# Seven half-size products for one group of weight columns in the first strip, with its operand sums made during the weight conversion

## The chip, the cores and the metric

The kernel runs on one core of one Trainium2 chip. The metric is the time of one execution on the device in microseconds (us). Engines: PE does matrix products into the PSUM banks, DVE, ACT and POOL work elementwise, SP issues transfers (DMA). Each engine works through its own queue in order, and waits at an instruction until what it needs has been signalled.

## The reference, cut to what matters

```python
# q, k, v: (8, 8, 576, 64)
kv = np.einsum('bhsd,bhse->bhde', k, v)
out = np.einsum('bhsd,bhde->bhse', q, kv)
x = out / np.sqrt(np.mean(out * out, axis=-1, keepdims=True) + 1e-06) * g_norm
x = x.transpose(0, 2, 1, 3).reshape(4608, 512)
h = x @ w_in                       # w_in: (512, 2048), 64-bit floats in memory
r = np.maximum(h, 0.0)
out = (r * r) @ w_out              # w_out: (2048, 512), 64-bit floats in memory
```

The weights lie in memory as 64-bit floats and are converted to 32 bits inside the kernel.

## The kernel before

The 4608 tokens are taken in nine strips of 512. For each strip there is a first product (x by w_in, then relu and square into four quarters of g, named 11, 12, 21, 22 in `gq`) and a second one (g by w_out). The attention part for the next strips (the slices that `attend` steps through) runs between the steps.

From the second strip on, products are done by Winograd's form of Strassen's method: 7 products of half-size blocks in place of 8, with sums of blocks as operands. The 7 products of one level are named 1 to 7 and run in the order `ORDER = (1, 2, 6, 5, 7, 3, 4)`; products 1, 6, 7 and 4 accumulate one after the other in bank A, 5 and 3 in bank B, 2 in bank C (`BANK`). Between them `combine` copies the bank on ACT (`snap`, after products 1, 6 and 5) or adds it to an earlier copy on DVE (after 2, 7 and 3), so that a later product into the same bank waits for that copy or sum.

The first strip is different, because its weights are only just arriving. w_in's columns come in four groups (g = 0 to 3). For each group and strip 0 the first product is done plainly, in 4 steps of `up_first`: 4 accumulating matmuls of 128x512 (8 records in the profile, two for each 32-bit matmul), after which ACT drains the bank with a relu and two squares. Four banks rotate (pool `fpsum`).

Beside these 16 steps the weights are converted, pair by pair. A piece is 512 KB of 64-bit numbers in a place of `raw_pool` (two pieces, a pair, to a place). Its way: load by SP (line 248), two ACT operations (`act_words`, lines 260 and 262, of 128x1024), one POOL operation (line 282), two DVE operations (lines 284 and 288). Words between the steps are in pool `wtmp`. `convert_pair(n)` issues the ACT part of pair n+1 ahead, then POOL's and DVE's part of pair n, then further loads, up to `AHEAD` pieces in advance. Pairs 0 to 7 are w_in (two to a group), pairs 8 to 15 w_out; pairs 12 to 15 have four further DVE sums each (`sums_out`), which are stored to memory. `PACE[i]` says how many conversions have been issued after step i. So ACT's queue mixes the drains of steps with the conversions, in the order of the program.

After the 16 steps the pools of the conversion are closed, the pools `stream` and `sum` are opened in their place, and strip 0's second product follows, one level of 7 products (`down`, order 1, 2, 5, 6, 7, 3, 4; lines 865 and 870 are the helpers that issue matmuls). Its operands come from the quarters of g, sums of them made by DVE, and weights partly read back by the transfers `w_blk<-w_out`. During it `sums_in(g)` makes the sums of w_in's blocks for the second strip, with line 316's scaling on ACT and four DVE operations in place (s1, s2, s4 into `w_s`, and a11 - a21 over a21).

Of the kernel before, what the change touches and what calls it, by code (L numbers as in the profile page):

```python
# [10 lines left out]
FP32 = mybir.dt.float32  # L11
# [3 lines left out]
AF = mybir.ActivationFunctionType  # L15
ALU = mybir.AluOpType
# [4 lines left out]
def kernel(  # L21
# [34 lines left out]
    nc = tc.nc  # L56
    P = 128
# [13 lines left out]
    TH = STRIP // 2  # L71
# [4 lines left out]
    SQ = 32  # L76
    Q_ON_PE = 2
    BEHIND = 1.6
    X_ON_PE = 2
    EPS = 1e-6  # L80
    AHEAD = 10
    PACE = (3, 4, 4, 5, 6, 7, 8, 9, 10, 11, 12, 13, 13, 14, 15, 16)
    const = ctx.enter_context(tc.tile_pool(name="const", bufs=1))
    wpool = ctx.enter_context(tc.tile_pool(name="wpool", bufs=1))
# [3 lines left out]
    xn_pool = ctx.enter_context(tc.tile_pool(name="xn", bufs=3))  # L88
    small = ctx.enter_context(tc.tile_pool(name="small", bufs=3))
    g_pool = ctx.enter_context(tc.tile_pool(name="g", bufs=4))  # L90
    dram = ctx.enter_context(tc.tile_pool(name="dram", bufs=1, space=bass.MemoryType.DRAM))
    c_pool = ctx.enter_context(tc.tile_pool(name="c", bufs=6))
    conv = ExitStack()
    xt_pool = conv.enter_context(tc.tile_pool(name="xt", bufs=1))
    raw_pool = conv.enter_context(tc.tile_pool(name="raw", bufs=5))
    spare_pool = conv.enter_context(tc.tile_pool(name="spare", bufs=1))
    wtmp = conv.enter_context(tc.tile_pool(name="wtmp", bufs=2))
    psums = ExitStack()
    fpsum = psums.enter_context(tc.tile_pool(name="fpsum", bufs=4, space=bass.MemoryType.PSUM))
    opening = ExitStack()  # L100
# [116 lines left out]
    KH, FH, DH = NP // 2, d_ff // 2, d_model // 2  # L217
    FQ = FC // 2
    WN = 512
    NG = FQ // 2  # L220
# [3 lines left out]
    block = lambda b: w_in[:, :, :, b] if b < 4 else w_s[:, :, :, b - 4]  # L224
# [14 lines left out]
    raw = []  # L239
# [65 lines left out]
    def minus(eng, out, a, b):  # L305
        eng.tensor_tensor(out=out, in0=a, in1=b, op=ALU.subtract)  # L306
# [3 lines left out]
    def pieces_in(i):  # L310
        g, k = divmod(i // 2, KH)
        convert_pair(i // 2, w_in[:, k, g].rearrange("p (a b) e -> p a (b e)", a=2))

    def sums_in(g):

        nc.scalar.activation(w_in[:, :, g, 0:4], w_in[:, :, g, 0:4], AF.Copy, scale=g_col)
        a11, a21, a12, a22, s1, s2, s4 = (block(b)[:, :, g] for b in range(7))
        nc.vector.tensor_tensor(out=s1, in0=a21, in1=a22, op=ALU.add)
        minus(nc.vector, s2, s1, a11)
        minus(nc.vector, s4, a12, s2)  # L320
        minus(nc.vector, a21, a11, a21)
# [57 lines left out]
    qT, kvd, x_n, xt = {}, {}, {}, {}  # L379
# [207 lines left out]
        if i == len(ns) - 1 and r:  # L587
            queried.pop()

    first = {}  # L590
    TAG_UP = "ABAC"


# [94 lines left out]
    xc = {}  # L688
# [2 lines left out]
        return xt[s][:, ts(th, TH // SQ), ts(kh, KH), :]  # L691

    def sums_x(s):
        xc[s] = t1, t2, t3, t4 = [
            sum_pool.tile([P, TH // SQ, KH, SQ], FP32, name=f"x_t{i}", tag="sum") for i in range(4)
        ]
# [170 lines left out]
    def product(p, i, lhsT, rhs, n):  # L867

        for k in range(n):
            nc.tensor.matmul(  # L870
                bank[BANK[p]][:, i, :], lhsT=lhsT(k), rhs=rhs(k),
                start=p in (1, 5, 2) and i == 0 and k == 0, stop=k == n - 1, skip_group_check=True,
            )

    def combine(p, c11, c12, c21, c22):

        b = bank[BANK[p]]
        if p in (1, 6, 5):
            snap[p] = c_pool.tile([P, 2, 2 * P], FP32, name=f"snap{p}", tag="c")
            nc.scalar.copy(snap[p], b)  # L880
        elif p == 4:
            c21(b)
        else:
            other, c = {2: (1, c11), 7: (5, c22), 3: (6, c12)}[p]
            c(b, snap[other])

    def quarters(s, g):

        if (s, 11) not in gq:
            for q in (11, 12, 21, 22):  # L890
                gq[s, q] = g_pool.tile([P, FQ, TH], FP32, name="gt", tag="gt")
        return {q: gq[s, q][:, 2 * g : 2 * g + 2, :] for q in (11, 12, 21, 22)}
# [27 lines left out]
    def up(s, g, p):  # L920
        open_bank(p)
        rhs = {
            1: halves(s, 0, 0), 2: halves(s, 1, 0), 3: halves(s, 1, 1),
            4: xc[s][3], 5: xc[s][0], 6: xc[s][1], 7: xc[s][2],
        }[p]
        for i in range(2):
            product(p, i, lambda kc: block(A_IN[p])[:, kc, g, ts(i, P)], lambda kc: rhs[:, :, kc, :], KH)
        dest = quarters(s, g)

        def relu_squared(q):  # L930
            def f(b, a):
                o = dest[q]
                nc.vector.tensor_tensor(out=o, in0=b, in1=a, op=ALU.add)
                nc.vector.scalar_tensor_tensor(out=o, in0=o, scalar=0.0, in1=o, op0=ALU.max, op1=ALU.mult)
            return f

        def last(b):
            nc.scalar.activation(dest[21], b, AF.Relu)
            nc.scalar.activation(dest[21], dest[21], AF.Square)

        combine(p, relu_squared(11), relu_squared(12), last, relu_squared(22))
# [417 lines left out]
    for s in range(N_STRIP):  # L1359
# [7 lines left out]
        if s >= DEEP_UP:  # L1367
            steps = [(0.5, up_slot, (s, slot)) for slot in range(55)]
        elif s == 0:
            steps = [(2, up_first, (g, fh, i)) for g in range(NG) for fh in range(2) for i in range(2)]  # L1370
        else:
            steps = [(1, up, (s, g, p)) for g in range(NG) for p in ORDER]
        n_up = len(steps)
# [9 lines left out]
                goal = min(pair_ends, key=lambda end: abs(end - goal))  # L1383
        total, done = sum(w for w, _, _ in steps), 0
        for i, (w, fn, a) in enumerate(steps):
            if s == 0 and i < n_up:
# [10 lines left out]
                if i == 14:  # L1397
                    for b in range(2):
                        store_first(b)
            elif s == 0 and i == n_up:  # L1400
                convert(len(conversions))
                conv.close()

                stream_pool = ctx.enter_context(tc.tile_pool(name="stream", bufs=6, reuse_waits="tile"))
# [56 lines left out]
            n = i + 1 - (n_up - 6)  # L1461
# [41 lines left out]
```

## Time and profile before

| | us |
|---|---|
| median of 3 runs | 869.34 |
| the runs | 869.1, 869.34, 873.36 |
| the profiled execution | 868.8 |
| its span, first to last instruction | 867.0 |
| PE busy in it | 857.8 |
| DVE, ACT, POOL busy | 702.0, 348.9, 328.1 |

The span is what the profile's views divide up; the execution's own time has 1.8 us beside it. The granted PE clock is 1.00 throughout. In the views a line gives the start in us, the duration in us, the engine, the line of the kernel, the operation, output<-input, shape and count, and in brackets the idle time before it with what ended it. Line numbers are those of the kernel before.

### The profile page before, as it was taken

To read this page: it belongs to the slowest core of one execution; us is meant where nothing else is said; L and a number is where in the kernel's file an instruction comes from. 1 tells how busy PE (TensorE), PEld (TensorE's weight loads), DVE (VectorE), ACT (ScalarE), POOL (GpSimd) and SP (SyncE) were. 2 spreads that over 40 slices of the span, in tenths; PEclk is the share of its full clock that TensorE was granted. 3 is DMA by queue.
4 is the path that set the end of the run, shared out by engine and by line. 5 is a ranking of instruction groups with operands and counts; after the bars stand their busy time and mean duration, and the time that the engine had idled before them with its cause. 6 is when DMAs were issued, how large, how long until landed. Compare 5 with 4: busy or idle time off the path is not lost.

```text
span 867.0 us, 32426 instructions
## 1 busy us (share of the span) xinstructions
PE 857.8 (99%) x14176; PEld 804.2 (93%) x14176; DVE 702.0 (81%) x1132; ACT 348.9 (40%) x777; POOL 328.1 (38%) x335
## 2 busy tenths in 40 slices
PE   7999999999999999999999999999999999999998
PEld 6445888889999999999999999999999999999998
DVE  3768988879877996789688967897889777975887
ACT  4888241320048303750356034901491148102810
POOL 1223004630458223730574045704470447145700
PEclk9999999999999999999999999999999999999999
DMA  9898998999999997989698979987678856885583
GB/s 307 277 362 269 274 377 239 295 332 353 280 264 259 342 325 233 228 307 344 209 244 273 341 239 281 283 297 270 198 236 302 301 165 221 293 282 196 175 315 121
DMA packets 169469, 236.46 MB, mean 273 GB/s; under 512 B 78704, under 2 KB 133744, under 8 KB 161008
## 3 DMA queue, kind: packets, MB, share of 16 engines
q1 hardware_dynamic: 169024, 234.33, 83.5%
q8 instruction: 111, 1.82, 0.9%
q14 instruction: 30, 0.25, 0.1%
q10 hardware_dynamic: 304, 0.07, 0.0%
HBM read 197.66 MB, written 36.70 MB: 270 GB/s over the span
## 4 chain that ended last, share of the span: by engine, by line
PE 83%; DMA 7%; DVE 5%; ACT 3%; SPq 1%; issue 1%; DVEq 0%; ACTq 0%
PE ps_A L865 36%; PE ps_B L865 31%; PE ps_C L865 5%; PE ps_A L870 4%; DMA raw<-in_moe_w_in_dram 2%; PE kv_ps L448 2%; PE x_ps L484 2%; PE ps_B L870 2%; DVE w_t L306 1%; DMA w_deep<-w_t 1%; DMA raw<-in_moe_w_out_dram 1%; DMA w_blk<-w_deep 1%; PE ps_C L870 1%; DMA first_qkv<-in_v_dram 1%; ACT w_c L260 1%
## 5 line engine op out<-in xcount | busy, mean ns | idle before, releaser
L865 PE MATMUL ps_B<-w_blk,g_s 128*64 128x128 f32 x2016 | 122.0, 273 | 0.0
L865 PEld LDWEIGHTS ps_B<-w_blk,g_s 128*64 128x64 f32 x2016 | 112.6, 137 | 0.1
L306 POOL TENSOR_TENSOR x_l<-xT 128x256 f32<-128x256 f32 x21 | 16.2, 773 | 230.2 <-PE ps_A L865 230.2
L865 PE MATMUL ps_B<-w_blk,gt 128*64 128x128 f32 x1504 | 94.1, 273 | 0.3 <-DMA w_blk<-w_deep 0.3
L865 PE MATMUL ps_A<-w_blk,g_s 128*64 128x128 f32 x1536 | 92.2, 273 | 0.0
L1323 POOL TENSOR_TENSOR snap<-snap,gt 128x512 f32<-128x512 f32 x35 | 46.2, 1320 | 112.5 <-ACT snap L1328 93.6
L865 PEld LDWEIGHTS ps_A<-w_blk,g_s 128*64 128x64 f32 x1536 | 85.7, 137 | 0.0
L865 PEld LDWEIGHTS ps_B<-w_blk,gt 128*64 128x64 f32 x1504 | 84.6, 137 | 0.8 <-PE ps_B L865 0.5
L1328 ACT COPY snap<-ps_A 128x512 f32<-128x512 f32 x63 | 36.8, 585 | 103.6 <-PE ps_A L865 96.2
L1263 ACT ACTIVATE gt<-gt 128x512 f32<-128x512 f32 x112 | 70.2, 627 | 9.9 <-DVE gt L1323 9.9
L1264 ACT ACTIVATE gt<-gt 128x512 f32<-128x512 f32 x112 | 70.7, 631 | 3.5
L865 PE MATMUL ps_A<-w_blk,gt 128*64 128x128 f32 x1152 | 71.2, 273 | 0.0
L865 PEld LDWEIGHTS ps_A<-w_blk,gt 128*64 128x64 f32 x1152 | 64.7, 137 | 0.0
L1112 ACT COPY o_sb<-ps_A 128x128 f32<-128x128 f32 x24 | 6.4, 265 | 144.7 <-PE ps_A L865 109.4
L306 DVE TENSOR_TENSOR gt<-gt 128x2048 f32<-128x2048 f32 (+1 forms) x29 | 59.7, 2063 | 0.0
L1111 DVE TENSOR_TENSOR o_sb<-o_sb,ps_B 128x256 f32<-128x256 f32 (+1 forms) x123 | 47.4, 386 | 14.3 <-ACT o_sb L1112 9.5
L865 PE MATMUL ps_A<-x_l,w_in 128*64 128x128 f32 x896 | 58.6, 273 | 0.2 <-DVE gt L1323 0.2
L1323 POOL TENSOR_TENSOR gt<-gt,snap 128x512 f32<-128x512 f32 x42 | 52.5, 1279 | 15.1 <-DVE snap L1323 15.1
L865 PEld LDWEIGHTS ps_A<-x_l,w_in 128*64 128x64 f32 x896 | 50.8, 137 | 0.5 <-DVE gt L1323 0.5
L865 PE MATMUL ps_B<-x_l,w_blk 128*64 128x128 f32 x784 | 51.2, 273 | 0.0
L865 PE MATMUL ps_A<-x_l,w_blk 128*64 128x128 f32 x784 | 51.2, 273 | 0.0
L1112 ACT COPY o_sb<-ps_B 128x128 f32<-128x128 f32 x31 | 8.2, 265 | 96.3 <-PE ps_B L865 96.3
(214 smaller groups left out, 1900.2 us busy)
## 6 DMA issues: line engine op xcount, KB each, us to landing
w_blk<-w_deep SPq DMA_DIRECT2D x56, 1024.0 KB, 7.3
w_blk<-w_out SPq DMA_DIRECT2D x56, 768.0 KB, 6.2
w_blk<-w_in_deep SPq DMA_DIRECT2D x49, 768.0 KB, 5.8
raw<-in_moe_w_in_dram SPq DMA_DIRECT2D x16, 512.0 KB, 9.2
raw<-in_moe_w_out_dram SPq DMA_DIRECT2D x16, 512.0 KB, 8.0
k<-in_k_dram SPq DMA_DIRECT2D x29, 256.0 KB, 4.9
v<-in_v_dram SPq DMA_DIRECT2D x29, 256.0 KB, 5.2
x_d<-x_q SPq DMA_DIRECT2D x27, 256.0 KB, 4.8
```

The source lines that it names most:

```text
L260: nc.scalar.activation(c, high_f, AF.Copy, scale=EXPONENT)
L306: eng.tensor_tensor(out=out, in0=a, in1=b, op=ALU.subtract)
L448: nc.tensor.matmul(ps[ts(h, D), i], lhsT=a, rhs=w, start=i == 0 and c == 0, stop=c == C, skip_group_check=True)
L484: nc.tensor.matmul(ps[half, r, i, ts(p, D)], lhsT=q[row, half], rhs=kvd[b, p][row, row], start=True, stop=True)
L865: nc.tensor.matmul(ps[half], lhsT=lhsT[:, half], rhs=rhs, start=start, stop=stop, skip_group_check=True)
L870: nc.tensor.matmul(bank[BANK[p]][:, i, :], lhsT=lhsT(k), rhs=rhs(k), start=p in (1, 5, 2) and i == 0 and k == 0, stop=k == n - 1, skip_gro ...
L1111: add = lambda out, a, b: nc.vector.tensor_tensor(out=out, in0=a, in1=b, op=ALU.add)
L1112: yield nc.scalar.copy(q[:, 3:4], small(1))
L1263: nc.scalar.activation(o, o, AF.Relu)
L1264: nc.scalar.activation(o, o, AF.Square)
L1323: add = lambda eng, out, a, b: eng.tensor_tensor(out=out, in0=a, in1=b, op=ALU.add)
L1328: nc.scalar.copy(t, ps)
```

## The change

Group 2 (`HALVED`) of strip 0's first product is done as seven products instead of four plain steps. Its operands: the four sums of x (`sums_x(0)`) are issued after step 1 and lie in the place where group 3's g will be; the three sums of the group's weights (`first_sums_in`) are issued after step 5, lie in the place of group 2's own g, and a21 is overwritten by a11 - a21 at once, so that `sums_in(2)` later makes its sums from that with three DVE operations. The relu and square of quarter 12 are on ACT instead of DVE.

With 7 steps in place of 4 there are 19 steps; `TURN` maps each to a turn of the former 16, by which the conversions (`PACE`) and other work are placed. A turn that occurs twice issues no conversion the second time: so there is none right after the last step ahead of the group, none after products 2 and 7, and none after the first step of group 3. Inside the group, after products 1, 6, 5, 3 and 4, the conversions of pairs 8, 9, 10, 11 and 12 are issued, each with the ACT part of the pair behind it.

The raw places go from 5 to 6 and the pieces in advance from 10 to 12, the places for words from 2 to 3. The pool `c` (copies of banks and output tiles) is opened only after the conversion; until then copies use the pool `xn`.

```diff
+    HALVED = 2
+    TURN = (*range(7), 6, 7, 7, 8, 9, 9, 10, 11, *range(12, 16))
-    AHEAD = 10
+    AHEAD = 12
-    c_pool = ctx.enter_context(tc.tile_pool(name="c", bufs=6))
     conv = ExitStack()
+    raw_pool = conv.enter_context(tc.tile_pool(name="raw", bufs=6))
     xt_pool = conv.enter_context(tc.tile_pool(name="xt", bufs=1))
-    raw_pool = conv.enter_context(tc.tile_pool(name="raw", bufs=5))
-    wtmp = conv.enter_context(tc.tile_pool(name="wtmp", bufs=2))
+    wtmp = conv.enter_context(tc.tile_pool(name="wtmp", bufs=3))
...
+    def first_sums_in(g):
+        a11, a21, a12, a22 = (block(b)[:, :, g] for b in range(4))
+        dest = quarters(0, g)
+        first_w[:] = s1, s2, s4 = [dest[q] for q in (22, 12, 21)]
+        nc.vector.tensor_tensor(out=s1, in0=a21, in1=a22, op=ALU.add)
+        minus(nc.vector, s2, s1, a11)
+        minus(nc.vector, s4, a12, s2)
+        minus(nc.vector, a21, a11, a21)
...
     def sums_in(g):
+        if g == HALVED:
+            minus(nc.vector, s2, a22, a21)
+            nc.vector.tensor_tensor(out=s1, in0=s2, in1=a11, op=ALU.add)
+            minus(nc.vector, s4, a12, s2)
+            return
...
     def sums_x(s):
+        if s:
+            ts_x = [sum_pool.tile(...) for i in range(4)]
+        else:
+            free = quarters(0, HALVED + 1)
+            ts_x = [free[q] ... for q in free]
...
     def combine(p, c11, c12, c21, c22):
         if p in (1, 6, 5):
+            pool, tag = (xn_pool, "x_n") if in_conversion else (c_pool, "c")
...
     def up(s, g, p):
+            w = first_w[b - 4] if s == 0 and b > 3 else block(b)[:, :, g]
...
                 nc.vector.tensor_tensor(out=o, in0=b, in1=a, op=ALU.add)
+                if s == 0 and q == 12:
+                    nc.scalar.activation(o, o, AF.Relu)
+                    nc.scalar.activation(o, o, AF.Square)
+                    return
...
         elif s == 0:
-            steps = [(2, up_first, (g, fh, i)) for g in range(NG) for fh in range(2) for i in range(2)]
+            for g in range(NG):
+                if g == HALVED:
+                    steps += [(1, up, (s, g, p)) for p in ORDER]
+                else:
+                    steps += [(2, up_first, (g, fh, i)) for fh in range(2) for i in range(2)]
...
+                c_pool = ctx.enter_context(tc.tile_pool(name="c", bufs=6))
...
             fn(*a)
             if s == 0 and i < n_up:
-                convert(PACE[i])
+                if i == 1:
+                    sums_x(0)
+                if i == 5:
+                    first_sums_in(HALVED)
+                convert(PACE[turn])
```

More of the change, by code (lines that the diff above doesn't have):

```diff
@@ L312, in pieces_in @@
         convert_pair(i // 2, w_in[:, k, g].rearrange("p (a b) e -> p a (b e)", a=2))
+    first_w = []
+    def first_sums_in(g):
[6 more added lines that the diff above has]
+        minus(nc.vector, a21, a11, a21)
     def sums_in(g):
@@ L588, in scaled_heads @@
             queried.pop()
-    first = {}
+    first, in_conversion = {}, [True]
     TAG_UP = "ABAC"
@@ L693, in sums_x @@
     def sums_x(s):
-        xc[s] = t1, t2, t3, t4 = [
-            sum_pool.tile([P, TH // SQ, KH, SQ], FP32, name=f"x_t{i}", tag="sum") for i in range(4)
-        ]
+        if s:
+            ts_x = [sum_pool.tile([P, TH // SQ, KH, SQ], FP32, name=f"x_t{i}", tag="sum") for i in range(4)]
+        else:
+            free = quarters(0, HALVED + 1)
+            ts_x = [
+                free[q].rearrange("p i t -> p (i t)").rearrange("p (a k t) -> p a k t", k=KH, t=SQ) for q in free
+            ]
+        xc[s] = t1, t2, t3, t4 = ts_x
         x = lambda kh, th: halves(s, kh, th)
@@ L878, in combine @@
         if p in (1, 6, 5):
-            snap[p] = c_pool.tile([P, 2, 2 * P], FP32, name=f"snap{p}", tag="c")
+            pool, tag = (xn_pool, "x_n") if in_conversion else (c_pool, "c")
+            snap[p] = pool.tile([P, 2, 2 * P], FP32, name=f"snap{p}", tag=tag)
             nc.scalar.copy(snap[p], b)
@@ L926, in up @@
         for i in range(2):
-            product(p, i, lambda kc: block(A_IN[p])[:, kc, g, ts(i, P)], lambda kc: rhs[:, :, kc, :], KH)
+            b = A_IN[p]
+            w = first_w[b - 4] if s == 0 and b > 3 else block(b)[:, :, g]
+            product(p, i, lambda kc: w[:, kc, ts(i, P)], lambda kc: rhs[:, :, kc, :], KH)
         dest = quarters(s, g)
@@ L1369 @@
         elif s == 0:
-            steps = [(2, up_first, (g, fh, i)) for g in range(NG) for fh in range(2) for i in range(2)]
+            steps = []
+            for g in range(NG):
[3 more added lines that the diff above has]
+                    steps += [(2, up_first, (g, fh, i)) for fh in range(2) for i in range(2)]
         else:
@@ L1385 @@
         for i, (w, fn, a) in enumerate(steps):
+            turn = (TURN[i] if i < n_up else i - n_up + 16) if s == 0 else None
             if s == 0 and i < n_up:
@@ L1396 @@
                         load_q_rest(b, nc.sync)
-                if i == 14:
+                if turn == 14:
                     for b in range(2):
@@ L1402 @@
                 conv.close()
+                in_conversion.clear()
                 stream_pool = ctx.enter_context(tc.tile_pool(name="stream", bufs=6, reuse_waits="tile"))
+                c_pool = ctx.enter_context(tc.tile_pool(name="c", bufs=6))
                 sum_pool = ctx.enter_context(tc.tile_pool(name="sum", bufs=8, reuse_waits="tile"))
@@ L1460 @@
                 sums_x(1)
-            n = i + 1 - (n_up - 6)
+            n = turn + 1 - 10
             pairs, m = divmod(max(n - 2 * NP, 0), 3)
```

## The prediction

> **What bounds the kernel.** I read the page's totals first, then PE's waits after the opening, then the stages around the change, the timelines of ACT, PE and DVE there, and the chain of waits.
>
> ```profile
> span 867.0 us, 32426 instructions
> PE 857.8 (99%) x14176; PEld 804.2 (93%) x14176; DVE 702.0 (81%) x1132; ACT 348.9 (40%) x777; POOL 328.1 (38%) x335
> ```
>
> PE is busy for 857.8 of 867.0 us. Its waits from 100 us on:
>
> ```profile
> PE ps_A L865 <- ACT snap L1328: 0.6, 1, 0.6
> PE ps_A L870 <- DVE o_sb L1042: 0.5, 1, 0.5
> PE ps_B L865 <- DMA w_blk<-w_deep: 0.3, 1, 0.3
> PE ps_A L865 <- DVE gt L1323: 0.2, 1, 0.2
> ```
>
> These 1.6 us are all that PE idles in the last 767 us, so PE time that the change takes out or adds in the first strip moves the end one for one, except at the second row: there PE catches up with DVE. The two stages after the point of change (the columns are PE, PEld, DVE, ACT, POOL, clock, DMA share, GB/s):
>
> ```profile
> 60.00:70.00 10.00, 9.78 (x44) 4.39 (x42) 7.20 (x6) 9.90 (x17) 3.92 (x3) 1.00 0.94 362
> 70.00:80.00 10.00, 9.93 (x47) 5.08 (x48) 9.70 (x10) 9.80 (x22) 2.78 (x3) 1.00 0.69 212
> ```
>
> Here ACT is as full as PE, and from 70 us DVE is too. ACT's timeline (start, duration):
>
> ```profile
> 50.49 0.60 ACT L916 ACTIVATE ps_A<-ps_A 128x512 f32<-128x512 f32 x1
> 51.12 0.66 ACT L918 ACTIVATE gt<-ps_A 128x256 f32<-128x256 f32 x2
> 53.38 1.14 ACT L260 ACTIVATE w_c<-raw 128x1024 f32<-128x1024 f32 x1 [1.60 <-DVE w_in L288]
> ...
> 57.53 1.16 ACT L260 ACTIVATE w_c<-raw 128x1024 f32<-128x1024 f32 x1 [0.78 <-DMA raw<-in_moe_w_out_dram]
> 58.58 1.15 ACT L262 ACTIVATE raw<-raw 128x1024 int32<-128x1024 uint32 x1
> 59.61 0.60 ACT L916 ACTIVATE ps_A<-ps_A 128x512 f32<-128x512 f32 x1
> ```
>
> PE's timeline:
>
> ```profile
> 51.08 3.60 PE L911 MATMUL ps_A<-xT,w_in 128*128 128x512 f32 x8
> 99.88 3.62 PE L870 MATMUL ps_B<-w_s,g_s 128*128 128x256 f32 x16
> 131.24 1.13 PE L870 MATMUL ps_A<-w_blk,gt 128*128 128x256 f32 x4 [0.46 <-DVE o_sb L1042]
> ```
>
> At 50.49 ACT drains the bank that PE left at 47.65, and at 59.61 the one that PE left at 54.51: ACT runs 3 to 5 us behind PE. That is free before, because four banks rotate. And PE is 0.46 us ahead of DVE at 131.24. The chain of waits says the same: from 81.05 to 131.24 it runs through DVE (and one store of w_t, 104.94 to 115.36).
>
> **PE's work.** Group 2 was 4 steps of 8 records. A step is 3.43 us (next start at 54.51 after 51.08), so 13.73. Seven products are 7 x 8 = 56 records of 256 columns; 16 of these take 3.45 (99.88 to 103.33), so a product takes 1.73 and the group 12.07. Saved: 1.66 us. A 512-column record is 0.429 us and a 256-column one 0.216, exactly half. The Trainium skill (TensorE: Matmul & The Clock Gate, section Back-to-back issue gap) speaks against this change: it states 81 ns for 128 columns and 131 ns for 512 in a stream where every matmul has its own weight load, so a narrow matmul would cost more than its share. By that ratio (0.62 for a quarter of the columns, an estimate from that page) the group would take at least 14.9 us, 1.2 more than before; the rows of line 870 in this trace disagree.
>
> **DVE's new work.** sums_x(0): 4 operations of 0.69 (L306, 128x512) right after the conversion that ends at 32.58; DVE then idles 2.99 us, so nothing. first_sums_in: 4 x 0.65 after pair 5's conversion at 46.06; the next begins at 47.47, so later conversions slip by about 1 us and catch up in the 0.93 and 2.31 us gaps behind: nothing, with up to 0.7 more if POOL's conversion overlaps (one L306 row is 1.41 beside a POOL row). Without that cover, 2.7 each. The combining adds 5 operations of 0.69 between pairs 8 and 12 (3.4 us), where DVE is 5.06 and 7.20 of 10 busy. One subtraction less for group 2 in the second strip (0.69) lies behind 131.24: nothing.
>
> **ACT's new work.** Out go 4 drains of 1.18 (59.61 to 60.78), 4.7; in come 3 copies at 0.47 spacing (0.59 long) and 4 activations of 128x512, about 0.55 apart (L1263: 627 ns long), 3.6. But the copies are now on PE's path. Products 1, 6 and 7 accumulate in one bank, 5 and 3 in another: 6 waits for the copy of 1, 7 for that of 6, 3 for that of 5, and 4 for DVE's sum that reads 7. Before each of these PE has one product (1.73) of cover, while ACT's queue, in order, holds a conversion of 2.1 us and its load.
>
> **Loads.** Pair n is two 512 KB pieces. With AHEAD 12 and six places, pair 5 goes ahead of the ten small q, k, v loads (SP 21.0 to 33.4), and pairs 8 and 9 go ahead of more_qkv and q_rest. The DMA share is at 1.0 from 40 to 68 us, so bytes ahead set the landing: pair 8 lands at about 51 instead of 53.2 (issue 45.8 plus 7.4), pair 9 at about 56 instead of 57.4, pair 10 with the same bytes ahead as before at 60.0 (50.9 plus 9.1), pair 11 at 62.6 (53.3 plus 9.3). Bounds for these: 1.5 us to either side, about one piece.
>
> **The walk through group 2**, by queue order. Product 1 51.08 to 52.81, product 2 to 54.53. ACT: pair 8 51.67 to 53.77, last drain to 54.95, copy of 1 to 55.54. Product 6 waits 1.1, runs 55.6 to 57.3; product 5 to 59.05. ACT: pair 9 from its landing 55.95 to 58.05, copy of 6 to 58.64; product 7 does not wait, and runs to 60.8. ACT: pair 10 from 60.15 to 62.2, copy of 5 to 62.8; product 3 waits 2.1, runs 62.85 to 64.6. DVE has pair 10 behind ACT and POOL to 64.95, then the sum that reads 7 to 65.6; product 4 waits 0.6 behind the query transposes (0.44) and ends at 67.4. Waits: 3.8 us against 1.66 saved. The former wait of 0.29 on the copy of qT at 70.07 goes, because ACT is by then no longer late. PE reaches the second product about 1.5 us late, near 84.5 instead of 83.06.
>
> DVE: sum for 3 to 66.9, ACT squares it to 68.05 and only then takes pair 12, before at 67.35; DVE's pair 12, before at 70.09, begins 0.4 to 0.7 later, and DVE is full from there to 109. At 131.24 DVE is late by 0.4 to 0.7, PE by 1.5 less its 0.46 of slack: 1.0. The later one counts: 868.8 + 1.0 = 869.8 us. The profiled execution took 868.8, 1.8 outside its span of 867.0, and lies 0.06% under the median of 869.34; the runs reach from 869.1 to 873.36. A measurement tells 0.5% (4.3 us) from no change.
>
> What stays hidden: xT's first write to its new place waits for stores of wt, issued by 96.9 and 3.5 us to landing, against ACT at 103.97. The c, stream and sum pools now open where the conversion's pools were, and their other first writers wait only for PE and DVE work that is over by then. From the second product on the queues of both programs are alike, but for the one subtraction.
>
> **Rivals.**
> *The saving is kept.* If pairs 9 and 10 land 1.5 us earlier, ACT is never behind a load: product 3 waits 0.5, product 4 0.7, product 6 still 1.1, so PE is 0.3 us early instead of late. Pair 12 is then taken at 66.65, DVE's chain is 1.0 us early, and at 131.24 PE's 0.3 and its 0.46 are realised: 868.8 - 0.7 = 868.1. For it: two more pieces in flight. Against: the DMA share is already 1.0. Even without any wait, DVE's chain caps it near 1 us: 867.8. Chance 0.27.
> *Slower: loads push the copies.* The dip of the DMA share to 0.37 at 30 to 32 us (small loads) moves behind pair 5, and if pair 10 then lands 3 us later, ACT's conversion holds the copy of 5, product 3 and DVE's pair 10 for 3 us more, all on PE's path: 869.8 + 3 = 872.8. It decides from a landing at 58.4 on, us for us, and passes 0.5% at about 63.5. For it: ACT waited for loads at 53.38 and 57.53 before. Against: total bytes are the same. Chance 0.13.
> *Narrow matmuls run long.* Each record has its own weight load, 190 ns in the PEld rows. Were that not hidden behind a 256-column record, it would cost 0.216 + 0.190 = 0.406 us, the group 22.7 instead of 12.07, and the kernel 869.8 + 10.7 = 880.5. The pace of line 870, with the same loads, speaks against it: 0.02. By the ratio of the Trainium skill's page on TensorE, named above, the same rival would cost 2.8 us instead (an estimate).
> *It does nothing.* PE's saving and waits cancel and DVE's chain is not moved: 868.8, chance 0.05.
>
> **Numbers.** My case has 0.53. Its own range, with landings 1.5 us either way, is 868.1 to 871.4. The range of 867.8 to 872.3 takes in the kept saving and most of the later loads, and the 0.5 us by which a median can lie over a profiled run. Faster by over 0.5% needs more than the 1.66 plus 0.46 there is: 0.02. Slower by over 0.5% is half of the slow rival: 0.07. Within: 0.91.
>
> **What would show it.** In the changed profile: 56 records of 256 columns at 0.216 in group 2; PE waits on ACT's copies ahead of products 6 and 3 of about 1 and 2 us, and on DVE ahead of product 4; pair 10's first ACT row near 60.15; the second product starting near 84.5; at 131 no wait of PE on DVE. If product 3 does not wait, or the second product starts before 83, the walk is wrong; if waits appear after 110 us that were not there, the reading that only the first strip changes is wrong.

## The result, and the profile after

The changed kernel took 874.28 us (median of 20 runs, 869.19 to 880.3) beside 869.65 us for the kernel before (20 runs, 866.46 to 874.16). The ratio is 1.0046, 95% interval [1.003, 1.0062]. The forecast was 869.8 with a range up to 872.3, so the loss of about 4.6 us is over four times the 1.0 expected, and outside the range. The profiled execution took 874.32 us. Line numbers are now those of the changed kernel: 893 issues the products (870 before), 935 the plain steps (911), 904 the copies, 959 and 964 the sums that combine products, 285 and 289 the DVE part of a conversion (one more where an experiment's edit adds a line above them).

The page's totals after:

```profile
span 872.5 us, 32490 instructions
PE 858.5 (98%) x14200; PEld 810.3 (93%) x14200; DVE 714.6 (82%) x1144; ACT 348.4 (40%) x772; POOL 328.6 (38%) x335
```

PE's work should have shrunk by 1.66 us, but its busy time is 0.7 us longer, so the same work ran more slowly somewhere. The rest of the longer span is idle time. All waits of PE between 40 and 140 us, then the one between 30 and 50 us (total, times, longest):

```profile
PE ps_A L893 <- DVE gt L959: 2.7, 1, 2.7
PE ps_B L893 <- ACT snap L904: 1.7, 1, 1.7
```

```profile
PE ps_A L935 <- DVE w_in L289: 0.6, 1, 0.6
```

The first two are inside the halved group. The third is in the first step of the second group, and the kernel before had nothing there. PE's timeline through the halved group and to the second product:

```profile
50.55 1.89 PE L893 MATMUL ps_A<-xT,w_in 128*128 128x256 f32 x8
52.27 1.89 PE L893 MATMUL ps_C<-xT,w_in 128*128 128x256 f32 x8
...
60.99 1.99 PE L893 MATMUL ps_B<-xT,gt 128*128 128x256 f32 x8 [1.65 <-ACT snap L904]
...
66.13 3.19 PE L893 MATMUL ps_A<-gt,w_in 128*128 128x256 f32 x8 [2.70 <-DVE gt L959]
...
86.86 3.72 PE L893 MATMUL ps_A<-w_s,gt 128*128 128x256 f32 x16
```

Products start 1.72 us apart where nothing waits. Product 3 (60.99) waits 1.65 us for the copy of product 5, product 4 (66.13) waits 2.70 us for the sum that reads product 7, and then product 4 itself takes 3.19 us instead of 1.9. The stretches around it say why (sum; PE, PEld, DVE, ACT, POOL; granted clock; DMA share; GB/s):

```profile
63.00:66.00 3.00, 0.42 (x4) 0.18 (x2) 2.96 (x3) 0.06 (x1) 0.13 (x1) 1.00 1.05 406
66.00:67.00 1.00, 0.87 (x4) 0.74 (x5) 0.96 (x3) 0.00 (x0) 0.00 (x0) 0.89 1.06 412
67.00:68.00 1.00, 1.00 (x4) 0.82 (x3) 1.00 (x2) 0.57 (x1) 0.00 (x0) 0.50 1.05 406
...
70.00:71.00 1.00, 1.00 (x14) 0.69 (x11) 0.07 (x1) 1.00 (x2) 0.90 (x1) 0.91 0.11 35
```

From 63 to 66 us it is still 1.00, with PE idle for 2.6 of the 3; right behind the wait it falls to 0.50. The missing parts, 0.11, three times 0.50 (67 to 70) and 0.09, add up to 1.7 us of PE time, over a stage of about 3.4 us.

ACT (start, duration) shows where the first wait is from:

```profile
58.28 1.17 ACT L261 ACTIVATE w_c<-raw 128x1024 f32<-128x1024 f32 x1 [1.20 <-DMA raw<-in_moe_w_out_dram]
59.34 1.13 ACT L263 ACTIVATE raw<-raw 128x1024 int32<-128x1024 uint32 x1
60.36 0.58 ACT L904 COPY snap<-ps_B 128x512 f32<-128x512 f32 x1
```

Pair 10 lands at 58.28, its two operations stand ahead of the copy of 5, and that copy ends only at 60.94, though product 5 was done by 57.6. DVE shows the second:

```profile
59.04 1.22 DVE L285 SCALAR_TENSOR_TENSOR w_c<-w_c,raw 128x1024 int32<-128x1024 int32 x1
60.29 1.94 DVE L289 SCALAR_TENSOR_TENSOR w_s<-raw,w_c 128x1024 int32<-128x1024 int32 x1
62.16 2.05 DVE L285 SCALAR_TENSOR_TENSOR w_c<-w_c,raw 128x1024 int32<-128x1024 int32 x1
...
65.39 0.68 DVE L959 TENSOR_TENSOR gt<-ps_A,snap 128x512 f32<-128x512 f32 x1
```

DVE works without a gap through pair 9 (59.04 to 62.2) and pair 10 (to 65.5). The sum that reads product 7, which PE finished near 59.3, comes behind both. From 42.23 to 69.80 DVE is busy for 27.15 of 27.57 us; in the same stretch of the kernel before it was 17.15.

The third wait goes back to x's sums, but not through DVE's queue. POOL's one operation on the pair (the clip, line 282 before and 283 after):

```profile
34.49 1.04 POOL L282 TENSOR_SCALAR w_c<-w_c 128x1024 f32<-128x1024 f32 x1 [5.58 <-ACT w_c L260]
33.43 1.56 POOL L283 TENSOR_SCALAR w_c<-w_c 128x1024 f32<-128x1024 f32 x1 [5.61 <-ACT w_c L261]
```

After, DVE's four sums end at 34.10 and DVE then waits 0.93 us for POOL, whose clip takes 1.56 us beside those sums instead of 1.04.

**The balance.** Two rows of the kernel before, the start of the first group's last step and of the second product:

```profile
33.64 3.60 PE L911 MATMUL ps_C<-xT,w_in 128*128 128x512 f32 x8
83.06 3.72 PE L870 MATMUL ps_A<-w_s,gt 128*128 128x256 f32 x16
```

The opening of a run, before the change acts, ends at different times (33.64 in the profile before, 32.55 here, 31.41 to 33.78 over all profiles below), so I count from the start of the first group's last step (the 3.60 us row at 32.55 that writes ps_C; two expectations below call it the third step). To the second product it was 49.42 us before (83.06 less 33.64) and is 54.31 now (86.86 less 32.55): 4.89 longer. The rows give 1.65 + 2.70 + 0.56 of new waits, 1.7 of half clock, less the 1.66 saved and less the 0.29 wait that went: 4.66. To the last product of the strip it was 97.60 (131.24 less 33.64) and is 101.86 (134.41 less 32.55): 4.26 longer, because the kernel before had its 0.46 wait on DVE there and this one has none. That is nearly the loss of the medians. (The spans of the two profiles differ by 5.5 us: the opening is 1.09 shorter here, this stretch 4.26 longer, and the rest, behind the last product, 2.33 longer.)

Behind that, the profile after has 2.5 us of waits on the loads `w_blk<-w_deep` (1.3) and on "issue" (0.9 and 0.3). Such waits, 0.7 to 3.4 us in all, are in every profile below that has the change's pools, with and without the halved group, so I don't put them down to the halved group. The two profiles with the old pools (the kernel before and e10) have 0.3 and 0.6 us of them, all on `w_blk<-w_deep` and none on "issue". Whether the pools bring them is left open below.

### The profile page after: what moved, and what is told of

Read it like the earlier page. It is cut to its first block, busy times and chain, and to the rows that moved or that the text cites. A ratio compares the mean times of both kernels' runs of the same rounds, so it can differ in the third digit from the quotient of the medians.

```text
span 872.5 us, 32490 instructions
## 1 busy us (share of the span) xinstructions
PE 858.5 (98%) x14200; PEld 810.3 (93%) x14200; DVE 714.6 (82%) x1144; ACT 348.4 (40%) x772; POOL 328.6 (38%) x335
## 4 chain that ended last, share of the span: by engine, by line
PE 88%; DMA 6%; ACT 4%; issue 1%; DVE 1%; SPq 1%; ACTq 0%; DVEq 0%
PE ps_A L888 35%; PE ps_B L888 30%; PE ps_A L893 7%; PE ps_C L888 5%; PE ps_B L893 3%; PE kv_ps L466 2%; PE x_ps L502 2%; DMA raw<-in_moe_w_in_dram 2%; DMA w_blk<-w_deep 2%; PE ps_C L893 2%; DMA raw<-in_moe_w_out_dram 1%; PE ps_A L935 1%; ACT w_c L261 1%; ACT raw L263 1%; DMA q<-in_q_dram 1%
```

## The experiments

**My theory** after the result: the loss is PE's waits inside the halved group, caused by conversions ahead of its copies and sums in the in-order queues of ACT and DVE, and the half clock that a long wait sets off. **Rivals**: the new pools and the earlier loads cost it; the narrow matmuls or the added DVE work cost it by themselves. One table first. "To second" and "to last" are the spans from the first group's last step to the second product and to the last product of the strip, in each kernel's profile; "clock under 1" counts runs whose mean granted clock was below 1.000; the median is less that of the kernel before on the same chip in the same sitting. The ratio with its interval is as the record has it and need not have the sign of that difference. There were four sittings (e1 to e4, e5 to e7, e8 to e10, e11 and e12); the row of the kernel before has the clocks of the first, and in the others 7 of 29, 6 of 29 and 1 of 17 of its runs were under 1. The changed kernel's row is from a sitting of its own.

| kernel | to second | to last | median against before | ratio, 95% interval | clock under 1 |
|---|---|---|---|---|---|
| before | 49.42 | 97.60 | 0 | 1 | 8 of 32 |
| changed | 54.31 | 101.86 | +4.63 | 1.0046 [1.003, 1.0062] | 16 of 20 |
| e1 pools and loads only | 48.92 | 96.47 | -1.48 | 0.9983 [0.9964, 1.0002] | 1 of 12 |
| e2 filler before 4 | 52.63 | 100.18 | +3.80 | 1.005 [1.0027, 1.0073] | 5 of 12 |
| e3 sums first | 55.54 | 103.09 | +4.38 | 1.0054 [1.0037, 1.0072] | 9 of 9 |
| e4 clip on DVE | 53.38 | 100.93 | +1.46 | 1.0023 [0.9999, 1.0047] | 5 of 10 |
| e5 step between | 48.22 | 98.95 | -0.38 | 0.9994 [0.9973, 1.0016] | 2 of 12 |
| e6 filler before 3 and 4 | 52.81 | 100.36 | +3.98 | 1.0048 [1.0024, 1.0072] | 4 of 12 |
| e7 e5 and clip on DVE | 48.80 | 98.85 | -0.39 | 1.0002 [0.998, 1.0025] | 3 of 12 |
| e8 e5 and late deep sums | 48.33 | 96.43 | -0.43 | 0.9995 [0.9981, 1.0009] | 1 of 12 |
| e9 pair 10 later | 51.05 | 99.77 | +1.79 | 1.0024 [1.0011, 1.0037] | 2 of 12 |
| e10 before, late deep sums | 49.87 | 97.42 | -0.86 | 1.0002 [0.9985, 1.0019] | 4 of 12 |
| e11 e8 and x's sums later | 48.90 | 96.71 | +0.50 | 1.0008 [0.9995, 1.0022] | 1 of 12 |
| e12 copy of 5 first | 52.47 | 101.53 | +5.33 | 1.0057 [1.0038, 1.0076] | 4 of 6 |

The medians follow "to last" only within 2 us, and both ways (e4: 3.33 longer, but +1.46; e11: 0.89 shorter, but +0.50), so a difference of less than 2 us between two rows can't be read from the medians.

**e1: the pools and loads alone.** The third group is plain again.

```diff
-    TURN = (*range(7), 6, 7, 7, 8, 9, 9, 10, 11, *range(12, 16))
+    TURN = range(16)
...
-                if g == HALVED:
-                    steps += [(1, up, (s, g, p)) for p in ORDER]
-                else:
-                    steps += [(2, up_first, (g, fh, i)) for fh in range(2) for i in range(2)]
+                steps += [(2, up_first, (g, fh, i)) for fh in range(2) for i in range(2)]
...
-                if i == 1:
-                    sums_x(0)
-                if i == 5:
-                    first_sums_in(HALVED)
```

> Group 2 is done plainly in four steps as before, with the order of conversions of before; the six raw places, 12 pieces ahead, three word places and the late pool c of the change stay. Theory (the loss is made inside group 2: PE's waits and the clock drop behind them): as fast as the kernel before, 869.7 us within 1.5, ratio 1.000, no clock drop, second product at 83 us or earlier. Rival (the new places and the earlier loads make the later reads of weights wait): 2 us or more slower than before, with waits on w_blk after 140 us in its profile.

Between 30 and 140 us its profile has no wait of PE at all, and it is level with the kernel before or a little under it. The six places, the twelve pieces ahead and the moved pools cost nothing that the median shows, so they can't be the 4.6 us; that rival is out.

**e2: filler ahead of product 4.**

```diff
     def up(s, g, p):
         open_bank(p)
+        if s == 0 and p == 4:
+            keep_busy(apsum.tile([P, 2, 2, d_model // 2], FP32, name="x_ps", tag="x", bufs=1)[:, 0, 0, 0:P], 11)
```

> The changed kernel with 11 matmuls of the identity (about 2.4 us of PE) issued ahead of product 4, where PE waits 2.7 us for DVE. Theory (that wait drops the granted clock to 0.5 for 3.4 us, which costs 1.7 us beside the wait): clock 1.000 throughout, product 4 again 1.9 us long instead of 3.2, second product 1.5 to 2 us earlier than 86.9, time about 872.5, ratio 1.003. Rival (the clock row marks the wait and costs nothing of its own): unchanged at 874.3, ratio 1.005, or slower by the filler.

PE's timeline:

```profile
63.03 2.62 PE L410 MATMUL x_ps<-ident 128*128 128x128 f32 x22
65.50 1.99 PE L893 MATMUL ps_A<-gt,w_in 128*128 128x256 f32 x8
```

Product 4 takes 1.99 us behind the filler instead of 3.19 behind an idle PE, and the wait of 1.98 us ahead of product 3 that this profile has is not followed by half clock. In this profile the second product comes 1.68 us sooner than in the changed kernel. The median did not follow: +3.80, where 872.5 (ratio 1.003) was expected, with the clock still under 1 in 5 of 12 runs. The profile is that of the fastest of the 12 (870.6). Of its seven runs at clock 1.000 the mean is 872.8, 2.9 above such runs of the kernel before in this sitting, and the profile has 2.58 to the last product.

**e3: all sums and copies ahead of the conversions.** Pairs 9 and 10 are converted two steps later and pair 11 one; pair 12 stays.

```diff
-    TURN = (*range(7), 6, 7, 7, 8, 9, 9, 10, 11, *range(12, 16))
+    TURN = (*range(7), 6, 7, 7, 7, 7, 8, 9, 11, *range(12, 16))
```

> The changed kernel with the conversions of pairs 9 to 12 issued later: none after products 6 and 5, pair 9 after product 7, pair 10 after 3, pairs 11 and 12 after 4, so that the copies of 6 and 5 and the sum that reads 7 stand ahead of them in the queues of ACT and DVE. Theory (PE's waits come from conversions that stand ahead of copies and sums): no PE wait in group 2 above 0.5 us, no clock drop, second product at 80 to 82 us; the end gains less, since DVE's chain to 131 us stays: 868 to 870, ratio 0.998 to 1.001. Rival (the loss is not in group 2's queue order): ratio stays at 1.005.

The halved group ran without a wait, and the time came out level with the changed kernel's. PE after it:

```profile
72.61 1.12 PE L435 MATMUL t_ps<-ident,q 128*128 128x128 f32 x4 [5.55 <-ACT qT L440]
73.52 5.14 PE L935 MATMUL ps_B<-xT,w_in 128*128 128x512 f32 x8
```

The delayed conversions stand ahead of the copy of qT on ACT, so the wait comes back in one piece of 5.55 us, and the next plain step takes 5.14 us instead of 3.60. In this profile the clock falls to 0.50 while PE still waits, near 69.8, and is back only near 76.6. The expectation missed: ACT's and DVE's conversions have to be done in this stretch, and putting them off moves the wait.

**e4: the clip of pairs 8 to 11 on DVE.** On POOL it overlaps DVE's rows of 1.94 and 2.05 us (POOL rows at 59.52 for 1.64 and at 62.09 for 1.04).

```diff
-        deque(conversion(pair_words.pop(n), dest, nc.gpsimd), 0)
+        deque(conversion(pair_words.pop(n), dest, nc.vector if 8 <= n <= 11 else nc.gpsimd), 0)
```

> The changed kernel with the clip of pairs 8 to 11 (one operation of 128x1024 a pair) on DVE instead of POOL. Theory (POOL's operation blocks DVE's two-input operations beside it, rows of 1.94 and 2.05 instead of 1.22): all DVE conversion rows of these pairs fall to 1.22, against four clips added on DVE; if a clip takes 0.6, the sum that reads product 7 comes about 0.5 us earlier and PE's wait for it is near 2.2; if 1.2, it comes as late as before. Rival (the long rows have another cause): rows of 1.9 to 2.1 stay in pairs 8 to 10.

DVE for pair 10, and PE's product 4:

```profile
61.13 1.23 DVE L285 SCALAR_TENSOR_TENSOR w_c<-w_c,raw 128x1024 int32<-128x1024 int32 x1
62.39 1.23 DVE L289 SCALAR_TENSOR_TENSOR w_s<-raw,w_c 128x1024 int32<-128x1024 int32 x1
```

```profile
64.28 3.38 PE L893 MATMUL ps_A<-gt,w_in 128*128 128x256 f32 x8 [2.89 <-DVE gt L959]
```

The long rows are gone, so they were DVE blocked by POOL: the 0.69 us that a clip takes on DVE cost it about what the 0.72 to 0.83 us of blocking did. The Trainium skill (SBUF — State Buffer, section SBUF: two separate sides) says that a DVE operation with two SBUF inputs and a GpSimd one that reads SBUF lock each other out; these rows agree. The wait ahead of product 3 fell to 0.76 us. Counted from the first group's last step, the sum came 0.72 us sooner, but PE was at product 3 0.89 sooner too, so the wait ahead of product 4 stayed, with the sum still behind pair 10, and so did the half clock. The median is +1.46, 3.2 less than the changed kernel's in its own sitting, and the profiles show 0.93 of that; the rest is not explained. What the long rows cost by themselves is not shown, because the clips took their place on DVE.

**e5: a plain step of the fourth group between products 7 and 3.** The fourth group's weights (pairs 6 and 7) are there by then, and the fourth bank is free. Pair 10 goes behind product 7 (e9 below makes this second change alone). Along with the step, the query transposes come to stand ahead of product 3, and 0.73 us of the attention's matmuls ahead of product 4.

```diff
+    PAIRS = (3, 4, 4, 5, 6, 7, 8, 8, 9, 9, 10, 10, 11, 12, 12, 13, 14, 15, 16)
...
+            steps.insert(13, steps.pop(15))
...
-                convert(PACE[turn])
+                convert(PAIRS[i])
```

> One plain step of the fourth group (3.43 us of matmuls whose weights and x are long there) is put between product 7 and product 3 of the halved group, and pair 10 is converted behind product 7 instead of behind product 5. Theory (the loss is the 4.35 us that TensorE waits inside the group, and the 1.7 us of half clock that mostly follow): the copy of product 5 and the sum that reads 7 have 5.2 us to be done in, so no wait over 0.5 us stays in the group, the granted clock is 1.0 in at least 8 of 10 executions, the second product starts near 81 to 82.5 (86.86 in the changed kernel), and as the DVE chain to 131 had only about half a microsecond to give, the time is 868.5 to 870.5, level with the kernel before. Rival (the halved group costs by itself, in narrow matmuls or in the DVE work that it adds): the second product starts early, but the time stays at 872 to 874, with waits on DVE before 131. Second rival (the waits only move, as they did when the sums were put first): a wait of 2 us or more on ACT or DVE ahead of a later step, 873 to 875.

PE's timeline in the group, and at the end of the strip:

```profile
59.38 3.60 PE L936 MATMUL ps_A<-xT,w_in 128*128 128x512 f32 x8
...
63.25 1.89 PE L894 MATMUL ps_B<-xT,gt 128*128 128x256 f32 x8
...
65.80 1.99 PE L894 MATMUL ps_A<-gt,w_in 128*128 128x256 f32 x8
```

```profile
122.92 7.17 PE L894 MATMUL ps_B<-w_blk,gt 128*128 128x256 f32 x32 [1.21 <-DVE gt L308]
131.37 7.17 PE L894 MATMUL ps_A<-w_blk,gt 128*128 128x256 f32 x32 [1.27 <-DVE o_sb L1073]
```

This is the main finding. The same halved group, with the same matmuls, sums and copies, runs without a wait, product 4 takes 1.99 us, and the whole loss is gone (0.9994 beside 1.0046). So neither narrow matmuls nor the added DVE and ACT work cost 4.6 us by themselves; the waits and what follows them do. PE reaches the second product 1.20 us sooner than in the kernel before (48.22 against 49.42) and waits for DVE at 123 and 131, where the gain is lost: to the last product it is 98.95 against 97.60.

**e6: filler ahead of both product 3 and product 4** (7 and 11 calls' worth).

```diff
+        if s == 0 and p in (3, 4):
+            keep_busy(apsum.tile([P, 2, 2, d_model // 2], FP32, name="x_ps", tag="x", bufs=1)[:, 0, 0, 0:P], 7 if p == 3 else 11)
```

> The changed kernel with matmuls of the identity into an unused bank ahead of product 3 (14 records, about 1.65 us) and ahead of product 4 (22 records, about 2.6 us), which fill the two waits and change nothing else. If the half clock is a price of its own that the idle time sets off, the clock is 1.0 in at least 9 of 12 executions and the median falls from 874 to 871 to 872, the level of the changed kernel's own executions without a drop (871.4); the waits themselves stay as lost time. If the drop comes from something else, the clock stays at 0.998 or lower in half the executions or more and the median is 873.5 to 875.

```profile
66.23 1.99 PE L893 MATMUL ps_A<-gt,w_in 128*128 128x256 f32 x8 [0.71 <-DVE gt L961]
```

Product 4 starts when it did in the changed kernel (66.23 and 66.13) but runs at full clock, and the second product comes 1.50 us sooner, close to the 1.7 of the half clock. The runs are less clear: the clock was under 1 in 4 of 12, not in at most 3, and the median was no lower than the changed kernel's. To the last product its profile is 2.76 us longer than the kernel before's, so 873.1 would fit (870.34 in this sitting), and 874.32 was measured. The price of the half clock is seen in profiles; that the median falls by it is not shown.

**e7: e5 with the clip of pairs 8 to 11 on DVE.** The edits are those of e5 and e4.

> The kernel with the plain step between products 7 and 3, and besides the clip of pairs 8 to 11 on DVE instead of GpSimd (4 x 0.69 us more on DVE; its conversions beside a busy GpSimd took 1.94 to 2.05 us, with the clip on DVE 1.22). Theory: DVE gains about as much as it takes on, so the time is within 0.7 us of the kernel without this edit (868 to 870.5). Rival (DVE's own load sets the end of this stretch): 1 to 2 us more or less than that kernel, by which of the two is larger.

As expected, no difference to e5.

**e8: e5, with the deep weight sums of products 6 and 7 later on DVE.**

```diff
-            while deep_due and i not in (n_up + 1, n_up + 4, n_up + 12, n_up + 13):
+            while deep_due and i not in (n_up + 1, n_up + 4, n_up + 6, n_up + 8, n_up + 12, n_up + 13):
```

> The kernel with the plain step between products 7 and 3, and besides the deep weight sums of products 6 and 7 of the second product (two blocks of 4 x 0.6 us on DVE) each put behind the next sum that TensorE waits for. There TensorE came 2.2 to 2.4 us early to the second product, and gave it back in two waits on DVE: 1.21 at 122.9 and 1.27 at 131.4. Theory (that queue is what takes the gain): DVE then ends the quarter's sum near 120.5 and the output sum near 129.0, both before TensorE needs them, the last product of the strip starts near 129.0 (131.37; 131.24 in the kernel before), and the time is 867 to 868.5, 1.5 to 2.5 us under the kernel before. Rival (the 2.3 us are taken by the next thing behind: DVE's sums of x or of the input weights for the second strip, or a later load): a wait on DVE or a DMA of 1.5 us or more between 129 and 165, and a time of 869 to 870.5.

```profile
120.76 7.14 PE L894 MATMUL ps_B<-w_blk,gt 128*128 128x256 f32 x32
127.93 7.17 PE L894 MATMUL ps_A<-w_blk,gt 128*128 128x256 f32 x32
```

Both waits went, and the last product came 2.52 us sooner than in e5 (96.43 against 98.95), as the theory said: DVE's queue took the gain there. Against the kernel before it is 1.17 us ahead at that point. The runs show 0.43 of it, inside the interval; the profile has 2.7 us of "issue" waits on PE later on. The 867 to 868.5 us expected were narrowly missed.

**e9: the changed kernel with only pair 10 converted one product later.** The edit puts pair 10 behind product 7, so behind the sum that reads it in DVE's queue. Pair 11 stays behind product 3, where the changed kernel has it, though the expectation counts it as moved.

```diff
+    PAIRS = (3, 4, 4, 5, 6, 7, 8, 8, 9, 9, 10, 10, 11, 12, 13, 13, 14, 15, 16)
...
-                convert(PACE[turn])
+                convert(PAIRS[i])
```

> The changed kernel with the conversions of pairs 10 and 11 each one product later (10 behind product 7, 11 behind product 3 as before the qT transposes, 12 behind product 4), nothing else: the plain step is not put between. Theory (two waits, each with its own cause): the sum that reads product 7 stands ahead of pair 10 on DVE and ends near 61.5, so the wait ahead of product 4 falls from 2.70 to under 0.7; the wait of 1.65 to 2.0 ahead of product 3 (copy of 5 behind pair 10 on ACT) stays, the second product starts near 84 to 85, the clock is 1.0 in at least 8 of 12 executions, and the time is 870.5 to 872. Rival (what counts is TensorE's idle time in any place): the wait moves to the step behind, clock 0.998 in most executions, 873 to 875.

```profile
PE t_ps L436 <- ACT qT L441: 1.4, 1, 1.4
PE ps_B L894 <- ACT snap L905: 1.3, 1, 1.3
```

The wait ahead of product 4 is gone and the one ahead of product 3 stays, as expected; a third of 1.4 us appears on the copy of qT. No wait is above 1.4, the clock is at 1 in 10 of 12 runs, and of the 4.63 us of loss 1.79 are left. So the 2.70 us wait, with what follows it, was the larger part, as far as medians of two sittings can be compared.

**e10: the control, the deep weight sums later in the kernel before.** The edit is that of e8.

> The kernel before with only the same two blocks of deep weight sums put later on DVE: a control. There TensorE waits for DVE neither at 123 nor at 131 (the sums end 0.46 us or more ahead of it), so there is nothing to gain: within 0.5 us of the kernel before. If this alone is faster by 1 us or more, the gain of the kernel with both edits is not the halved group's.

No difference that can be measured, as expected: with 49.87 us to the second product and 97.42 to the last, it no longer has the wait of 0.46 at 131, but its wait on a copy of qT is 0.7 instead of 0.3.

**e11: e8, with x's sums behind step 2 instead of step 1.**

```diff
-                if i == 1:
+                if i == 2:
                     sums_x(0)
```

> The kernel with the plain step between products 7 and 3 and the later deep weight sums, and besides the sums of x for the first strip behind step 2 instead of step 1, so behind the DVE conversion of the next pair instead of ahead of it. In the changed kernel and every variant with those sums at step 1, TensorE waits 0.56 for that conversion in the first step of the second group (none in the kernel before). Theory: that wait goes, the time from the start of the first group's third step to the start of the second product falls from 48.33 to 47.6 to 48.0 (49.42 in the kernel before), and the time is 867.5 to 869 (0.4 to 0.6 under the kernel without this edit, which alone can't be told). Rival: the sums delay the next pairs by as much, and a wait of 0.5 or more appears ahead of the halved group.

The 0.56 us wait went: the first step of the second group takes 3.71 us to the next (35.32 to 39.03), as in the kernel before, against 4.26 (35.98 to 40.24) in the changed one. So x's sums did delay the conversion behind them; POOL's clip of that pair is back at 1.04 us here. To the second product it came out 0.57 longer than e8, with a wait of 1.22 us on ACT's kv_all where e8 had 0.5. The gain was not kept.

**e12: no step between, but an order in which the copy of 5 comes ahead of pair 10.** With the edits of e8 and e11 besides.

```diff
+    PAIRS = (3, 4, 4, 5, 6, 7, 8, 8, 9, 9, 9, 10, 11, 11, 12, 13, 14, 15, 16)
```

> The changed kernel without the step put between, but with an order of conversions made for the halved group: pair 9 behind product 5 (so that the copy of 5 stands ahead of pair 10 on ACT), pair 10 behind product 7 (so that the sum that reads 7 stands ahead of it on DVE), the later pairs one step on; the sums of x behind step 2 and the deep weight sums later as in the other kernel. Theory (order alone was the fault): no wait over 0.6 in the halved group, clock 1.0 in at least 9 of 12, the second product 47.5 to 49 us behind the first group's third step (54.31 in the changed kernel), 867.5 to 869.5. Rival (the group needs other work between its products, whatever the order): a wait of 1 us or more ahead of product 3 or 4 or of the transposes behind them, the second product 50 us or more behind, 870 to 872.

```profile
63.74 3.42 PE L894 MATMUL ps_A<-gt,w_in 128*128 128x256 f32 x8 [3.23 <-DVE gt L960]
```

Product 3 no longer waits, but product 4 waits 3.23 us and then runs at half clock: now pair 9's conversion, which this order had put later, stands ahead of the sum on DVE. The rival holds. While DVE and ACT work through a pair every 3 to 4 us, each of these orders left some pair ahead of a copy or a sum for which PE has 1.73 us of cover; e3, e9 and e12 each moved a wait, and the 3.43 us of other work in e5 covered it.

## Why the prediction was wrong

**What held.** A 256-column record takes 0.216 us and a product 1.73 (starts at 50.55 and 52.27). The rule from the Trainium skill (TensorE: Matmul & The Clock Gate, section Back-to-back issue gap) by which narrow matmuls would cost more than their share does not show here. The copies are on PE's path, and conversions in the queues make them late. DVE's sum stands behind pair 10. The 0.29 wait on qT went. At 131 PE no longer waits for DVE. The pools and loads cost nothing that e1's median shows. That DVE's chain caps any gain near 131 was confirmed by e5 and, with the cap lifted, by e8.

**The step that failed: the walk through group 2.** It had waits of 1.1, 2.1 and 0.6 us ahead of products 6, 3 and 4, together 3.8; measured were 0, 1.65 and 2.70, together 4.35. In the sum of waits this is only 0.55 us, but the wait ahead of product 4 is the one that the half clock stands behind. Count from the start of product 1 (51.08 in the walk, 50.55 in the profile). PE was ready for product 4 after 12.88 us instead of 13.96, because pairs 8 to 10 came 1.0 to 1.3 us sooner to ACT and the wait ahead of product 6 fell away. The sum that product 4 waits for ended after 15.52 us instead of 14.52.

For that sum the walk took DVE as free as soon as POOL had pair 10 ready; in the profile DVE was still at pair 9, and pair 10's first row took 2.05 us instead of 1.23, beside a POOL row. So this overlap was wrong: DVE's new work was priced at nothing because DVE had gaps, with 0.7 us allowed for one row beside POOL. The gaps were POOL's time. With DVE full, one row in each of pairs 6 to 10 ran 0.72 to 0.84 us long (1.94 to 2.06 instead of 1.22), about 4 us together. Besides, the walk's own rows give 1.8 us to the second product and not 1.5: product 4 ends at 67.4 where the plain steps ended at 65.35, less the 0.29.

**The term that was missing: the clock.** Nothing in the prediction priced a fall of the granted clock behind a wait, and the waits that it forecast were all 2.1 us or less. The profile has 1.7 us of PE time in it, and 16 of the 20 runs had a mean clock under 1, against 8 of 32 of the kernel before (in another sitting). The four runs of the changed kernel with the clock at 1.000 average 871.4 us, the 24 such runs of the kernel before 869.9: 1.5 apart, near the forecast's 1.0. Runs sorted in this way may differ in more than the clock (in the kernel before, without the halved group, the eight under 1 average 2.7 us above the 24), and the fillers did not lower the median, so this only fits the reading.

**The term that was taken at nothing: x's sums.** "DVE then idles 2.99 us, so nothing" counted 4 x 0.69 = 2.8 us into a gap of 2.99, and DVE was indeed done in time. But in that gap POOL's clip of the next pair had run alone; beside the sums it took 1.56 us instead of 1.04, the conversion began 0.56 us later (counted from the first group's last step), and PE waited 0.56 us for it. e11 took that wait away.

**The rivals.** The kept saving did not happen, though its condition nearly did: pairs 9 and 10 came 1.0 and 1.3 us sooner to ACT, but PE came sooner too, and the two waits stayed; e5 shows what it needed. Late loads did not happen: they came early. The reading that only the first strip changes is in doubt by the prediction's own sign: waits appear after 110 us that the kernel before doesn't have (1.2 us on "issue", 1.0 more on `w_blk<-w_deep`).

**What stays open.** How much of the median the half clock alone makes; the filler kernels ended 1.2 us above what their profiles up to the last product of the strip would give. And why e8 and e11, 1.17 and 0.89 us ahead at the last product of the strip, were not measurably faster than the kernel before. The pools may have a part in that: from the last product to the end the two profiles with the old pools take 735.8 and 735.9 us, the other twelve 736.0 to 740.0. But e1, the kernel with 740.0, is not slower in its median, and no run settles it. No kernel here beats that one measurably; e8, at -0.43, beats the changed kernel, at +4.63, by 5.1 us.

## What to carry to other kernels

Cutting a step into products that share banks puts each copy and each sum on the matmul engine's path: before counting the saved matmuls, compare the cover between dependent products with the longest thing that can stand ahead of them in the in-order queues, and look for independent matmuls to put between. Reordering the queues alone moved waits each time here (e3, e9, e12), and only e9 came out faster by it. The gaps of one engine may be the time in which another works: here DVE's were POOL's, and filling them made rows of both longer. A wait can cost more than its length: behind the one of 2.70 us the half clock took another 1.7. And a gain that gets through has still to be followed to the next engine that has no slack.

## What the runs showed of the hardware

The granted clock fell to 0.50 for about 3.4 us around the end of waits of 2.70 (changed kernel), 2.89 (e4) and 3.23 us (e12), and for about 6.8 us from within the wait of 5.55 us (e3); in the profiles of e2 (1.98) and e9 (1.33 and 1.36) it stayed at 1.00. The Trainium skill (TensorE: Matmul & The Clock Gate, section What's actually happening) puts the return to half clock at an idle window of about 3.4 us, in windows that run freely. The length of the stage agrees with that, but here 2.70 us of idle, with 1.65 us of another wait a little ahead of it, were enough, and not in every run.

DVE's conversion rows of 128x1024 took 1.22 us alone and 1.94 to 2.06 beside a POOL row, and POOL's clip took 1.04 us alone and up to 1.67 beside DVE rows.
